# phi(K) as one maximum in place of a clamp and a sum, in a linear attention and GLU block

## The chip, the cores and the metric

One core of a Trainium2 chip. The time is the device time of one execution in microseconds (us); the median of several runs counts. The engines of the core work side by side, each through its own list of instructions in order: TensorE (PE; PEld is its loading of weights), VectorE (DVE), ScalarE (ACT), GpSimd (POOL) and SyncE (SP), which issues transfers. They wait for each other by semaphores.

## The reference

Two pre-norm residual blocks on x of 1 x 2048 x 448, bf16: linear attention with 16 heads of 28, then a gated GELU layer of width 1792.

```python
phi = lambda t: jnp.where(t > 0, t + 1, jnp.exp(t)) + 1e-6
pq, pk = phi(q), phi(k)
kv = jnp.einsum("bhsd,bhse->bhde", pk, v)
z = jnp.einsum("bhsd->bhd", pk)
num = jnp.einsum("bhqd,bhde->bhqe", pq, kv)
den = jnp.einsum("bhqd,bhd->bhq", pq, z)[..., None] + 1e-6
h = x + (num / den) @ wo                  # q, k, v from layernorm(x) @ wqkv
h2 = h + (gelu(g) * u) @ w_down           # g, u from layernorm(h)
```

## The kernel before

The 2048 rows are 16 tiles of 128 rows; tile t holds every 16th row. The program writes down tasks, each with an engine, the buffers it reads and writes, and a name; the five strings of ORDERS give, as task numbers, the order of the tasks on each engine, and waits are derived from the buffers. Where one instruction has several waits, the table HOLD can say whose wait stands first. An instruction never overtakes another on its engine, so a waiting instruction holds up all that stands behind it there.

**Normalization.** For each tile VectorE takes the statistics (L413, L414) and ScalarE the reciprocal deviation (L420, with the pointer eps_t as bias, and L422, without a pointer). The normalized tile xnn has 512 columns: 448 of data and 64 that hold 1.0. The first four tiles are transposed by TensorE with the matrix ident (L443), the others by a transfer (L455), into xnT: four blocks of 128 rows, where rows 64 to 127 of the last block are the ones.

**K and Q tiles.** Task k_t is four matmuls of 448 columns (L469) into one of four PSUM banks that K and Q tiles take in turn; a bank is free again when its tile was read. The weights wqk_sb have zeros in rows 64 to 127 of their last block (L364), so the ones add nothing. ek_t (L480, ScalarE) writes e1 = exp(K); ck_t (L481, VectorE) clamps e1 to between 0 and 1 + 1e-6, in place; pk_t (L482, VectorE) writes max(K, 1e-6) + e1, which is phi(K), to pk in bf16. q_t is the same projection for Q; ScalarE writes exp and relu of it (eq_t L496, rq_t L497), and VectorE later makes phi(Q) of them (cq L564, aq L565).

**P.** The matmuls of L488 multiply xnn, transposed, with pk, and sum over all tiles in four more banks: P = xnn^T pk, 448 rows and one of ones, which gives z. For tiles 10 and later they are split in two tasks: pt1_t, the bank with z, and pt3_t, the three others.

**From P to the output of the attention.** z1 (L514, ScalarE) and z0 (L515, VectorE) put z on all partitions of zbc; evpD_3 (L516, VectorE), evpA_0 and evpA_1 (L519, ScalarE) and evpD_2 (L521, VectorE) copy P to pt_sb in bf16. kv (L527, TensorE) needs all four copies; then kvm (L531), and the task w2 (L547) multiplies with wo; evwA (L551, ScalarE) and evwD (L553, VectorE) evacuate it. For the first two pairs of tiles the denominator goes through t1d or t1p (L569), dr (L572, VectorE), deA (L574, ScalarE, bias by the pointer eps_d), rd (L575) and pn (L576). For tiles 0 and 1 TensorE transposes the result (tro, L599), which takes the banks that w2 used.

The orders around this place, by names:

```
TensorE  ... k_15 pt1_11 pt3_11 pt1_12 pt1_13 pt3_12 pt1_14 pt1_15 pt3_13 pt3_14 pt3_15 q_5 q_4 kv q_7 q_8 w2_2 w2_0 w2_1 q_9 w2_3 tro_1 tro_0 q_6 ...
ScalarE  ... ek_14 ek_15 z1 evpA_0 evpA_1 deA_0 eq_5 eq_4 rq_5 deA_1 deA_2 eq_7 rq_4 deA_3 rq_7 evwA_0 evwA_2 rq_9 ...
VectorE  ... ck_15 pk_15 aq_3 cq_1 evpD_3 z0 aq_1 t1d_0 dr_0 evpD_2 rd_0 dr_1 dr_2 kvm rd_2 kvd dr_3 rd_1 pn_0 rd_3 pn_1 evwD_1 ...
```

**The GLU layer.** After the residual sum and the second normalization, tasks gu (L731, L733: gate and up side by side on half the rows each), ge (L751, gelu on ScalarE, writes gl), hm (L753, product on VectorE, writes hh) and down (L697, L678) follow in chunks of tiles to the end; two pairs of banks alternate for gu, so the third task, gu2_2, needs the first pair read by ge and hm.

Of the kernel before, what the change touches and what calls it, by code (L numbers as in the profile page):

```python
# [5 lines left out]
BF16 = mybir.dt.bfloat16  # L6
F32 = mybir.dt.float32
ALU = mybir.AluOpType
AF = mybir.ActivationFunctionType
# [39 lines left out]
)  # L49
HOLD = {  # L50
    66: (36,), 141: (140,), 165: (164,), 214: (213,), 216: (215,), 323: (302,), 326: (324,), 431: (340,), 704:
    (564,), 735: (734,), 781: (672,), 839: (836,), 849: (846,), 854: (852,), 866: (865,),
# [176 lines left out]
def bass_sequential_preLN__linear_attn_block__glu_gated_geglu__prompt_kernel(  # L229
    nc, A_x, A_wqkv, A_wo, B_x, B_w_gate, B_w_up, B_w_down, out  # L230
):
    S, D, FF, H, DH = 2048, 448, 1792, 16, 28
    T, P = S // 128, S // 256
# [4 lines left out]
    EPS_LN, EPS = 1e-5, 1e-6  # L238
    XN_R, PK_R, HN_R, HR = 10, 8, 4, 8
# [7 lines left out]
    G = _Graph()  # L247
    es = ExitStack()
    with es:
        block = es.enter_context(nc.Block())  # L250

        def sb(name, shape, dt):
            return es.enter_context(nc.sbuf_tensor(name, shape, dt))
# [28 lines left out]
        pk = sb("pk", [128, PK_R, D], BF16)  # L282
# [7 lines left out]
        eps_d = sb("eps_d", [128, 1], F32)  # L290
        rd = sb("rd", [128, 4, H], F32)
# [16 lines left out]
        b_xn = bufs("xn", XN_R)  # L308
# [7 lines left out]
        b_epsd = _Buf("epsd")  # L316
# [33 lines left out]
        def op(eng, fn, r, w, name, after=()):  # L350
            return G.add(eng, fn, r=r, w=w, name=name, after=after)
# [8 lines left out]
        def dma_x(q, a, b):  # L360
            return dma(q, x_sb[:, a:b, :], xv[:, a:b, :], b_x[a:b], "dx%d" % a)

        for dst, b, nm_ in ((wqk_sb, b_wpad[0], "wqkpad"), (wv_sb, b_wpad[1], "wvpad")):
            op("dve", lambda e, dst=dst: e.memset(dst[B_, 3, :], 0.0), [], [b], nm_)  # L364
        dma_x("sp", 0, 1)
# [17 lines left out]
        op("pool", lambda e: e.memset(eps_d[:], EPS), [], [b_epsd], "epsd")  # L383
        op("pool", lambda e: e.memset(mhalf[:], -0.5), [], [b_mhalf], "mhalf")
# [14 lines left out]
        def act_exp(fn, r, w, name):  # L399
            t_ = G.add("act", fn, r=r, w=w, name=name, after=[tbl1])  # L400
            exps.append(t_)
            return t_
# [69 lines left out]
        def proj_reads(t, b):  # L472
            return [(b_xnT[t][0], 0), (b_xnT[t][1], 2), (b[0], 0), (b[1], 3), (b_wpad[0], 3)]

        def k_tile(t):
            bk = slot()
            i, ip = t % 4, t % PK_R
            psK = ps[:, bk, 0:D]
            G.add("pe", lambda e, W: proj(e, W, t, bk, D), r=proj_reads(t, b_wk), w=[b_ps[bk]], name="k_%d" % t, mw=True)
            eks.append(act_exp(lambda e: e.activation(e1[:, i, :], psK, AF.Exp), [b_ps[bk]], [b_e1[i]], "ek_%d" % t))  # L480
            op("dve", lambda e: e.tensor_scalar(e1[:, i, :], e1[:, i, :], 1.0 + EPS, 0.0, ALU.min, ALU.max), [b_e1[i]], [b_e1[i]], "ck_%d" % t)  # L481
            op("dve", lambda e: e.scalar_tensor_tensor(pk[:, ip, :], psK, EPS, e1[:, i, :], ALU.max, ALU.add), [b_ps[bk], b_e1[i]], [b_pk[ip]], "pk_%d" % t)  # L482
            groups = ((3, 0, 1, 2),) if t < PT_SPLIT else ((3,), (0, 1, 2))
            for cs in groups:
                def fpt(e, cs=cs):
                    ins = None
                    for c in cs:
                        ins = e.matmul(ps[:, BK_PT[c], 0:D], xnn[:, t % XN_R, c * 128:(c + 1) * 128], pk[:, ip, :], start=(t == 0), stop=(t == T - 1))  # L488
                    return ins
                G.add("pe", fpt, r=[b_xn[t % XN_R], b_ones2, b_pk[ip]], w=[b_ps[BK_PT[c]] for c in cs], name="pt%d_%d" % (len(cs), t))  # L490
# [23 lines left out]
        op("act", lambda e: e.activation(zbc[B_, :], ps[B_, BK_PT[3], 0:D], AF.Identity), [b_ps[BK_PT[3]]], [b_z[1]], "z1")  # L514
        op("dve", lambda e: e.tensor_copy(zbc[A_, :], zbc[B_, :]), [b_z[1]], [b_z[0]], "z0")  # L515
        op("dve", lambda e: e.tensor_copy(pt_sb[A_, 3, :], ps[A_, BK_PT[3], 0:D]), [b_ps[BK_PT[3]]], [b_pt[3]], "evpD_3")  # L516
        for c in range(3):
            if c in (0, 1):
                op("act", lambda e, c=c: e.activation(pt_sb[:, c, :], ps[:, BK_PT[c], 0:D], AF.Identity), [b_ps[BK_PT[c]]], [b_pt[c]], "evpA_%d" % c)  # L519
            else:  # L520
                op("dve", lambda e, c=c: e.tensor_copy(pt_sb[:, c, :], ps[:, BK_PT[c], 0:D]), [b_ps[BK_PT[c]]], [b_pt[c]], "evpD_%d" % c)  # L521
# [301 lines left out]
```

## Time and profile before

| what | value |
|---|---|
| median of 3 runs | 190.59 us (190.52 to 190.61) |
| span of the profiled execution, first to last instruction | 188.3 us |
| granted TensorE clock in it | 1.000 |
| VectorE, busy in it | 129.3 us |
| ScalarE, busy in it | 76.5 us |

The span is that of one execution; a run's time also holds what lies before the first and after the last instruction. Views that follow: the *chain* goes back from the last instruction to what released each step (columns: start, us, what). The *timeline* gives start, us, engine, line, operation, out<-in and count, and in brackets the idle time before and what ended it; neighbouring instructions of a line are merged. *Windows* give, for a stretch, its length, then busy time and count of each engine, the granted clock, the transfer engines' busy share and GB/s. *Groups* give busy us, mean ns of one, and idle us before. *Waits* give us in total, times, and the longest.

### The profile page before, as it was taken

What the parts mean: (1) busy time and instruction counts of PE and PEld (TensorE: products, weight loads), DVE (VectorE), ACT (ScalarE), POOL (GpSimd) and SP (SyncE); (2) the same over time, 40 slices, a digit from 0 to 9 for tenths busy, and PEclk for the clock granted to TensorE, in tenths of its full rate; (3) what the DMA queues carried; (4) which work ended last, traced back from release to release, by engine and by line L of the source; (5) the groups of instructions that cost most, each with busy time, mean ns of one, the idle gap of its engine ahead of it and who ended that gap; (6) DMA issues with size and microseconds to landing.
All of it is one profiled execution on the core that took longest, in us unless ns stands there. A gap on an engine that the chain in (4) does not pass through costs nothing.

```text
span 188.3 us, 4459 instructions
## 1 busy us (share of the span) xinstructions
PE 184.3 (98%) x1813; PEld 109.2 (58%) x1813; DVE 129.3 (69%) x330; ACT 76.5 (41%) x220; POOL 50.0 (27%) x91
## 2 busy tenths in 40 slices
PE   7999999999999999999999999999999999999994
PEld 7545555555688788965554555555545545454554
DVE  4999959999899998786796762562645244335432
ACT  3878752799963231432234222321242222224100
POOL 6067910704505686033614000206100000000000
PEclk9999999999999999999999999999999999999999
DMA  5996458999393526820005720000096000002024
GB/s 169 387 231 88 96 104 194 218 222 174 65 320 64 95 52 116 84 52 0 0 3 98 144 54 0 0 3 2 3 135 111 3 0 24 3 0 98 3 79 140
DMA packets 35076, 17.11 MB, mean 91 GB/s; under 512 B 26864, under 2 KB 33648, under 8 KB 35056
## 3 DMA queue, kind: packets, MB, share of 16 engines
q1 hardware_dynamic: 34432, 16.32, 41.1%
q10 hardware_dynamic: 624, 0.52, 0.8%
q8 instruction: 14, 0.23, 0.5%
q14 instruction: 6, 0.05, 0.1%
HBM read 8.26 MB, written 1.84 MB: 54 GB/s over the span
## 4 chain that ended last, share of the span: by engine, by line
PE 94%; DVE 3%; DMA 1%; issue 0%
PE ps L733 38%; PE ps L697 19%; PE ps L469 12%; PE ps L731 9%; PE ps L488 6%; PE ps L627 3%; PE ps L678 3%; PE ps L628 2%; DMA x_sb<-in_A_x_dram 1%; DVE st L413 1%; PE ps L617 1%; PE ps L547 1%; PE ps L527 1%; PE ps L443 0%; PE ps L654 0%; DVE den L572 0%
## 5 line engine op out<-in xcount | busy, mean ns | idle before, releaser
L733 PE MATMUL ps<-hnT,wgu_sb 64*128 64x512 bf16 (+1 forms) x490 | 88.8, 333 | 0.0
L731 PE MATMUL ps<-hnT,wgu_sb 64*128 64x512 bf16 (+1 forms) x490 | 88.6, 333 | 0.0
L751 ACT ACTIVATE gl<-ps 128x256 bf16<-128x256 f32 x112 | 36.6, 383 | 85.3 <-PE ps L731 84.4
L753 DVE TENSOR_TENSOR hh<-ps,gl 128x256 bf16<-128x256 f32 x112 | 42.1, 416 | 41.4 <-ACT gl L751 41.3
L733 PEld LDWEIGHTS ps<-hnT,wgu_sb 64*128 64x128 bf16 x490 | 45.2, 94 | 32.9 <-DVE hh L753 3.4
L731 PEld LDWEIGHTS ps<-hnT,wgu_sb 64*128 64x128 bf16 x490 | 45.4, 94 | 2.5
L697 PE MATMUL ps<-wd_sb,hh 64*128 64x448 bf16 x392 | 41.5, 349 | 0.0
L697 PEld LDWEIGHTS ps<-wd_sb,hh 64*128 64x128 bf16 x392 | 23.2, 94 | 14.5
L469 PE MATMUL ps<-wqk_sb,xnT 128*128 128x448 bf16 x128 | 27.4, 353 | 0.0
L413 DVE BATCH_NORM_STATS2 st<-x_sb 128x6 f32<-128x448 bf16 x32 | 19.2, 612 | 1.8 <-DMA x_sb<-in_A_x_dram 1.7
L585 POOL TENSOR_TENSOR t<-pq,zbc 128x448 f32<-128x448 bf16 x12 | 12.3, 1042 | 23.7 <-DVE pq L583 22.0
L469 PEld LDWEIGHTS ps<-wqk_sb,xnT 128*128 128x128 bf16 x128 | 11.9, 98 | 11.4 <-DVE pk L482 0.8
L488 PE MATMUL ps<-pk,xnn 128*128 128x448 bf16 x64 | 13.9, 352 | 0.0
L627 PE MATMUL ps<-w,pqnT 64*128 64x448 bf16 x49 | 11.5, 349 | 0.1
L425 POOL TENSOR_SCALAR ln<-mv 128x2 f32<-128x2 f32 x7 | 2.0, 291 | 35.2 <-DVE mv L414 35.0
L480 ACT ACTIVATE e<-ps 128x448 bf16<-128x448 f32 x16 | 8.5, 539 | 5.6 <-PE ps L469 5.5
L628 PE MATMUL ps<-pt_sb,pqnT 64*128 64x448 bf16 x42 | 10.2, 350 | 0.0
L633 DVE TENSOR_TENSOR x_sb<-ps,x_sb 128x448 bf16<-128x448 f32 x16 | 9.6, 616 | 0.7 <-PE ps L628 0.6
L662 POOL TENSOR_SCALAR hn<-x_sb,nm,rs 128x448 bf16<-128x448 bf16 x14 | 9.9, 719 | 0.4
L482 DVE SCALAR_TENSOR_TENSOR pk<-ps,e 128x448 bf16<-128x448 f32 x16 | 9.8, 617 | 0.1
L488 PEld LDWEIGHTS ps<-pk,xnn 128*128 128x128 bf16 x64 | 6.3, 98 | 5.9 <-DVE pk L482 0.3
L453 POOL TENSOR_SCALAR xnn<-x_sb,nm,rs 128x448 bf16<-128x448 bf16 x12 | 8.9, 744 | 2.2 <-ACT rs L422 1.9
(85 smaller groups left out, 160.5 us busy)
## 6 DMA issues: line engine op xcount, KB each, us to landing
out_dram<-x_sb SPq DMA_DIRECT2D x15, 112.0 KB, 1.8
wd_sb<-in_B_w_down_dram SPq DMA_DIRECT2D x1, 1568.0 KB, 8.4
x_sb<-in_A_x_dram SPq DMA_DIRECT2D x3, 448.0 KB, 5.9
wgu_sb<-in_B_w_gate_dram SPq DMA_DIRECT2D x1, 896.0 KB, 12.1
wgu_sb<-in_B_w_up_dram SPq DMA_DIRECT2D x1, 896.0 KB, 16.5
wgu_sb<-in_B_w_gate_dram SPq DMA_DIRECT2D x1, 672.0 KB, 6.1
wgu_sb<-in_B_w_up_dram SPq DMA_DIRECT2D x1, 672.0 KB, 8.5
wo_sb<-in_A_wo_dram SPq DMA_DIRECT2D x1, 392.0 KB, 7.5
```

Source lines behind the costliest of these rows:

```text
L413: op("dve", lambda e: e.bn_stats(st[:, t, :], src_ap), [b_src], [b_st[t]], "bnst%s_%d" % (tag, t))
L469: ins = e.matmul(ps[:, bk, 0:D], xnT[:, t, k, :], wqk_sb[:, k, c0:c0 + D], start=(k == 0), stop=(k == 3))
L488: ins = e.matmul(ps[:, BK_PT[c], 0:D], xnn[:, t % XN_R, c * 128:(c + 1) * 128], pk[:, ip, :], start=(t == 0), stop=(t == T - 1))
L585: op("pool", lambda e, n=n: e.tensor_tensor(t1[:, n, :], pq[:, a + n, :], zbc[:, :], ALU.mult), [b_pq[a + n]] + b_z, [b_t1[n]], "t1p_%d" % ...
L627: e.matmul(ps[:, BK_OUT[0], 0:D], pqnT[ra, i2, sg // 2, :], w2[ra, sg // 2, :], start=(sg == 0), stop=(sg == 5))
L628: ins = e.matmul(ps[:, BK_OUT[1], 0:D], pqnT[rb, i2, 3 + (sg + 1) // 2, :], (w2 if sg == 6 else w2s)[rb, sg // 2, :], start=(sg == 0), sto ...
L662: op("pool", lambda e, t=t, sh=sh: e.tensor_scalar(hn[:, sh, 0:D], x_sb[:, t, :], nm2[:, t:t + 1], rs2[:, t:t + 1], ALU.add, ALU.mult), [b ...
L697: ins = e.matmul(ps[:, bko[half][n], 0:D], hh[rows, j, sl[n]], wd_sb[rows, j, :], start=(j == 0 and (half == 0 or p == 6)), stop=(j == NJ ...
L731: first = e.matmul(psG[:, jj * N:(jj + 1) * N], wgu_sb[A_, k, j * 128:(j + 1) * 128], hnT[A_, ka_, c0:c0 + N], start=(k == 0), stop=(k == ...
L733: ins = e.matmul(psU[:, jj * N:(jj + 1) * N], wgu_sb[B_, k, j * 128:(j + 1) * 128], hnT[B_, kb_, c0:c0 + N], start=(k == 0), stop=(k == NK ...
L751: G.add("act", lambda e, gi=gi, cs_=cs_, psG=psG: e.activation(gl[:, gi, cs_], psG[:, cs_], AF.Gelu_apprx_tanh), r=[b_ps[BK_G[i]]], w=[b_g ...
L753: op("dve", lambda e, dst=dst, srcU=srcU, srcL=srcL: e.tensor_tensor(dst, srcU, srcL, ALU.mult), [b_ps[BK_U[i]], b_glh], [b_ar[j_][t % HR] ...
```

## The change

K gets its 1 in the projection: row 64 of the last weight block, which meets a row of ones, is set to 1.0 for the K half (w1row). So PSUM holds K + 1; ek_t computes exp(K + 1 - 1) with the pointer neg1 as bias; and pk_t is max(min(e1, 1), K + 1) in one instruction, without the 1e-6. The sixteen ck_t are gone. The 1e-6 comes back where P is read: pk has two more columns that hold 1e-6, the matmuls of L488 take one of them along as column 449, and its sum is added to every column of P as P is evacuated, by a per-partition operand: on VectorE straight from PSUM (evpD_3, evpD_2), on ScalarE as a bias from the new buffer ecol, which VectorE copies out of PSUM; z gets 2048 x 1e-6 from eps_s. The orders of all engines stay; the new tasks stand as follows: w1row behind the two memsets on VectorE, ecol on VectorE between dr_0 and evpD_2, three memsets (neg1, pkeps, epss) in GpSimd's start. The task numbers of ORDERS shift, and HOLD now has some hundreds of entries, mostly the neighbouring task's.

```diff
-        pk = sb("pk", [128, PK_R, D], BF16)
+        pk = sb("pk", [128, PK_R, D + 2], BF16)
...
+        neg1 = sb("neg1", [128, 1], F32)
+        eps_s = sb("eps_s", [128, 1], F32)
+        ecol = sb("ecol", [128, 2], F32)
...
+        op("dve", lambda e: e.memset(wqk_sb[64:65, 3, D:2 * D], 1.0), [b_wpad[0]], [b_w1r], "w1row")
...
+        op("pool", lambda e: e.memset(neg1[:], -1.0), [], [b_neg1], "neg1")
+        op("pool", lambda e: e.memset(eps_s[:], S * EPS), [], [b_epss], "epss")
+        op("pool", lambda e: e.memset(pk[:, :, D:D + 2], EPS), [], [b_pke], "pkeps")
...
-            eks.append(act_exp(lambda e: e.activation(e1[:, i, :], psK, AF.Exp), [b_ps[bk]], [b_e1[i]], "ek_%d" % t))
-            op("dve", lambda e: e.tensor_scalar(e1[:, i, :], e1[:, i, :], 1.0 + EPS, 0.0, ALU.min, ALU.max), [b_e1[i]], [b_e1[i]], "ck_%d" % t)
-            op("dve", lambda e: e.scalar_tensor_tensor(pk[:, ip, :], psK, EPS, e1[:, i, :], ALU.max, ALU.add), [b_ps[bk], b_e1[i]], [b_pk[ip]], "pk_%d" % t)
+            eks.append(act_exp(lambda e: e.activation(e1[:, i, :], psK, AF.Exp, bias=neg1[:, 0:1]), [b_ps[bk], b_neg1], [b_e1[i]], "ek_%d" % t))
+            op("dve", lambda e: e.scalar_tensor_tensor(pk[:, ip, 0:D], e1[:, i, :], 1.0, psK, ALU.min, ALU.max), [b_ps[bk], b_e1[i]], [b_pk[ip]], "pk_%d" % t)
...
-                        ins = e.matmul(ps[:, BK_PT[c], 0:D], xnn[:, t % XN_R, c * 128:(c + 1) * 128], pk[:, ip, :], start=(t == 0), stop=(t == T - 1))
+                        ins = e.matmul(ps[:, BK_PT[c], 0:D + 1], xnn[:, t % XN_R, c * 128:(c + 1) * 128], pk[:, ip, 0:D + 1], start=(t == 0), stop=(t == T - 1))
...
-        op("act", lambda e: e.activation(zbc[B_, :], ps[B_, BK_PT[3], 0:D], AF.Identity), [b_ps[BK_PT[3]]], [b_z[1]], "z1")
+        op("dve", lambda e: e.tensor_copy(ecol[:, 0:2], ps[:, BK_PT[0]:BK_PT[0] + 2, D]), [b_ps[BK_PT[0]], b_ps[BK_PT[1]]], [b_ecol], "ecol")
+        op("act", lambda e: e.activation(zbc[B_, :], ps[B_, BK_PT[3], 0:D], AF.Identity, bias=eps_s[B_, 0:1]), [b_ps[BK_PT[3]], b_epss], [b_z[1]], "z1")
...
-        op("dve", lambda e: e.tensor_copy(pt_sb[A_, 3, :], ps[A_, BK_PT[3], 0:D]), [b_ps[BK_PT[3]]], [b_pt[3]], "evpD_3")
+        op("dve", lambda e: e.tensor_scalar(pt_sb[A_, 3, :], ps[A_, BK_PT[3], 0:D], ps[A_, BK_PT[3], D:D + 1], None, ALU.add), [b_ps[BK_PT[3]]], [b_pt[3]], "evpD_3")
...
-                op("act", lambda e, c=c: e.activation(pt_sb[:, c, :], ps[:, BK_PT[c], 0:D], AF.Identity), [b_ps[BK_PT[c]]], [b_pt[c]], "evpA_%d" % c)
+                op("act", lambda e, c=c: e.activation(pt_sb[:, c, :], ps[:, BK_PT[c], 0:D], AF.Identity, bias=ecol[:, c:c + 1]), [b_ps[BK_PT[c]], b_ecol], [b_pt[c]], "evpA_%d" % c)
...
-                op("dve", lambda e, c=c: e.tensor_copy(pt_sb[:, c, :], ps[:, BK_PT[c], 0:D]), [b_ps[BK_PT[c]]], [b_pt[c]], "evpD_%d" % c)
+                op("dve", lambda e, c=c: e.tensor_scalar(pt_sb[:, c, :], ps[:, BK_PT[c], 0:D], ps[:, BK_PT[c], D:D + 1], None, ALU.add), [b_ps[BK_PT[c]]], [b_pt[c]], "evpD_%d" % c)
```

More of the change, by code (lines that the diff above doesn't have):

```diff
@@ L15 @@
 ORDERS = (
[33 rows of a table removed]
[33 rows of a table added]
 )
 HOLD = {
-    66: (36,), 141: (140,), 165: (164,), 214: (213,), 216: (215,), 323: (302,), 326: (324,), 431: (340,), 704:
-    (564,), 735: (734,), 781: (672,), 839: (836,), 849: (846,), 854: (852,), 866: (865,),
[78 rows of a table added]
 }
@@ L315, in bass_sequential_preLN__linear_attn_block__glu_gated_geglu__prompt_kernel @@
             _Buf(n) for n in ("ident", "ones", "mones", "mtmp", "mask", "eps", "mhalf", "powtmp"))
-        b_epsd = _Buf("epsd")
+        b_epsd, b_epss, b_ecol, b_neg1, b_pke, b_w1r = _Buf("epsd"), _Buf("epss"), _Buf("ecol"), _Buf("neg1"), _Buf("pke"), _Buf("w1r")
         b_st1, b_mv1, b_nm1, b_ln1, b_rs1 = bufs("st1", T), bufs("mv1", T), bufs("nm1", T), bufs("ln1", T), bufs("rs1", T)
@@ L472, in proj_reads @@
         def proj_reads(t, b):
-            return [(b_xnT[t][0], 0), (b_xnT[t][1], 2), (b[0], 0), (b[1], 3), (b_wpad[0], 3)]
+            return [(b_xnT[t][0], 0), (b_xnT[t][1], 2), (b[0], 0), (b[1], 3), (b_wpad[0], 3)] + ([(b_w1r, 3)] if b is b_wk else [])
         def k_tile(t):
@@ L487, in fpt @@
                     for c in cs:
-                        ins = e.matmul(ps[:, BK_PT[c], 0:D], xnn[:, t % XN_R, c * 128:(c + 1) * 128], pk[:, ip, :], start=(t == 0), stop=(t == T - 1))
+                        ins = e.matmul(ps[:, BK_PT[c], 0:D + 1], xnn[:, t % XN_R, c * 128:(c + 1) * 128], pk[:, ip, 0:D + 1], start=(t == 0), stop=(t == T - 1))
                     return ins
-                G.add("pe", fpt, r=[b_xn[t % XN_R], b_ones2, b_pk[ip]], w=[b_ps[BK_PT[c]] for c in cs], name="pt%d_%d" % (len(cs), t))
+                G.add("pe", fpt, r=[b_xn[t % XN_R], b_ones2, b_pke, b_pk[ip]], w=[b_ps[BK_PT[c]] for c in cs], name="pt%d_%d" % (len(cs), t))
         def q_tile(t):
```

144 rows, old and new, of tables (HOLD, ORDERS) are left out of this document.

## The prediction

> **What bounds the kernel now.** I read the page's head and its chain of work first: who sets the end?
>
> ```profile
> span 188.3 us, 4459 instructions
> PE 184.3 (98%) x1813; PEld 109.2 (58%) x1813; DVE 129.3 (69%) x330; ACT 76.5 (41%) x220; POOL 50.0 (27%) x91
> PE 94%; DVE 3%; DMA 1%; issue 0%
> ```
>
> TensorE carries 94% of the chain that ended last. A busy share does not prove that matmuls run at their peak, so I took the stage where the removed instruction lives, between two points of the chain, by windows, and then the waits of TensorE there.
>
> ```profile
> 10.92:32.70 21.78, 21.78 (x117) 11.05 (x115) 19.26 (x56) 13.85 (x42) 10.58 (x26) 1.00 0.65 126
> PEld ps L469 <- DVE pk L482: 0.8, 3, 0.3
> PEld ps L488 <- DVE pk L482: 0.3, 2, 0.2
> ```
>
> 115 weight loads in 21.78 us are 189.4 ns for each 448-column matmul, 0.42 ns a column, at granted clock 1.00 and without a hole; the chain holds nothing but matmuls there. The 1.1 us in which weight loads waited for pk are waits of the loader, hidden behind the matmul in flight: they cost no matmul time. VectorE is busy for 19.26 of these 21.78 us and yet not the bound.
>
> The chain leaves TensorE once, where the sums P are evacuated:
>
> ```profile
> 30.61 2.09 PE ps L488 x11
> 32.73 0.62 DVE pt_sb L516
> 33.37 0.40 DVE zbc L515
> 33.79 0.39 DVE pq L565
> 34.19 0.55 DVE t L569
> 34.76 0.62 DVE den L572
> 35.38 0.54 DVE pt_sb L521
> 35.96 1.03 PE ps L527 x16
> 36.99 1.51 PE ps L469 x8
> ...
> 40.59 0.45 PE ps L599 x8
> ```
>
> TensorE finishes pt1_15 at 32.70; from there VectorE does evpD_3, z0, aq_1, t1d_0, dr_0, evpD_2 back to back, and kv starts at 35.96 when evpD_2 is done. The timeline says how much TensorE loses to this, and where ScalarE stands:
>
> ```profile
> 32.73 0.54 ACT L514 ACTIVATE zbc<-ps 64x448 f32<-64x448 f32 x1 [1.54 <-PE ps L488]
> ...
> 34.23 1.68 PE L469 MATMUL ps<-wqk_sb,xnT 128*128 128x448 bf16 x8
> ...
> 34.43 0.98 ACT L519 ACTIVATE pt_sb<-ps 128x448 bf16<-128x448 f32 x2 [1.16 <-PE ps L488]
> ...
> 35.29 0.61 DVE L521 CAST pt_sb<-ps 128x448 bf16<-128x448 f32 x1
> 35.41 0.31 ACT L574 ACTIVATE den<-den,eps_d 128x16 f32<-128x16 f32 x1
> ...
> 35.82 0.24 DVE L575 RECIPROCAL rd<-den 128x16 f32<-128x16 f32 x1
> ...
> 36.47 0.55 ACT L497 ACTIVATE pq<-ps 128x448 bf16<-128x448 f32 x1
> ```
>
> q_5 and q_4 keep TensorE busy to 34.23 + 1.68 = 35.91, and kv follows 0.05 us later: evpD_2 comes just in time, and evpA_0 and evpA_1 on ScalarE end at 35.41, half a microsecond early. That half microsecond is all the room the change has here.
>
> **The change part by part.** Durations come from these groups:
>
> ```profile
> L420 ACT ACTIVATE ln<-mv,eps_t 128x1 f32<-128x1 f32 x18 | 5.2, 294 | 2.2 <-DVE mv L414 2.0
> ...
> L481 DVE TENSOR_SCALAR e<-e 128x448 bf16<-128x448 bf16 x16 | 4.2, 271 | 2.3 <-ACT e L480 2.2
> ...
> L422 ACT ACTIVATE rs<-ln 128x1 f32<-128x1 f32 x18 | 3.4, 200 | 0.3
> ...
> L435 DVE TENSOR_SCALAR xnn<-x_sb,mv,rs 128x448 bf16<-128x448 bf16 x4 | 1.5, 377 | 0.1
> ...
> L647 DVE COPY hn<-hn 128x64 bf16<-128x64 bf16 x2 | 0.2, 142 | 0.0
> ```
>
> *Removed:* sixteen ck, 16 x 271 ns = 4.3 us of VectorE, all before 32.7 us. They pay nothing: TensorE runs there without a hole, and kv's chain starts at 32.73 from pt1_15, which TensorE reaches in its order after 11 matmuls (30.61 + 2.09), whether pk_15 is early or not. pk itself stays one pass over the same shapes.
>
> *Bias pointer on the sixteen ek:* an ACTIVATE of one column with a pointer bias (L420) takes 294 ns, without one (L422) 200. I take +94 ns for each, the functions being different; bounds 0 and 94. 16 x 94 ns = 1.5 us of ScalarE, while it is busy for 13.85 of 21.78 us, and pk, which follows ek, has lost the 271 ns of ck in between: nothing on the path. Without that room, each would delay pk by its 94 ns.
>
> *Weight row, memsets, 449th column:* w1row writes 448 elements of one partition; the zero memset of 448 words took 0.43 us.
>
> ```profile
> 1.18 0.43 DVE L364 MEMSET wqk_sb<- 64x448 uint32 x1
> ...
> 3.01 0.29 POOL L380 TENSOR_SCALAR_AFFINE_SELECT ident<-ones_bf 128x128 bf16<-128x128 bf16 x1
> ...
> 3.34 0.63 DVE L413 BATCH_NORM_STATS2 st<-x_sb 128x6 f32<-128x448 bf16 x1 [1.73 <-DMA x_sb<-in_A_x_dram]
> ...
> 5.25 0.27 PEld L443 LDWEIGHTS ps<-ident,xnn 128*128 128x128 bf16 x4
> ```
>
> It ends near 2.1 us, inside the 1.73 us in which VectorE waits for x; uncovered it would cost its 0.43. GpSimd's three small memsets lie among its start-up work, whose first urgent result is ident: ready at 3.30, first used by TensorE at 5.25, so 1.95 us cover them. 64 matmuls of 449 columns instead of 448: 64 x 0.42 ns = 0.03 us on the path.
>
> *The evacuations.* This is what matters. evpA_0 and evpA_1 now take their bias from ecol, and ecol stands on VectorE behind dr_0 and ahead of evpD_2. So ScalarE, in order, cannot start evpA_0 at 34.43. Step by step:
> - evpD_3 reads its addend through a pointer. L435 with two pointers takes 377 ns against 271 for L481 with none: 53 ns a pointer, bounds 0 and 0.1. z1, 94 ns longer, ends at 33.36, before evpD_3 (33.40), so z0 goes by evpD_3. ecol's turn: 35.29 + 0.05 = 35.34.
> - ecol itself, two columns out of PSUM, is in no row. The small copy L647 gives 0.14, the reciprocal of 16 columns (0.24, above) the other bound; I take 0.15, since it is a copy: 35.49.
> - To ScalarE 0.05 (evpD_2 ended at 35.90, kv started at 35.96): 35.54.
> - Two evacuations 0.98, plus 2 x 0.094 for the pointers: 1.17. They end at 36.71; kv at 36.77 instead of 35.96: **+0.81 us**. evpD_2, ended near 36.1, is no longer what kv waits for.
>
> *The table HOLD* reorders waits that stand before one instruction; the last to hold decides in either order: 0, or one hand-over of 0.05 us where it does not.
>
> The Trainium skill (VectorE: DVE Perf Modes, section on the TRN2 errata) gives (120 + columns) cycles at 0.96 GHz from PSUM to SBUF, an estimate of 0.13 us for ecol; by it kv would start 0.02 us sooner. No run here shows such a small copy yet.
>
> *What is queued behind.* ScalarE starts deA_0 at 36.71 instead of 35.41, 1.30 late; rd_0 on VectorE waits for it (36.71 + 0.31 + 0.04 = 37.06, 1.24 late), and everything behind it on VectorE. Rows of what follows (the timeline, then ScalarE's window with its busy time second, the first gelu, hm, and gu2_2 in the chain):
>
> ```profile
> 37.93 0.61 DVE L572 TENSOR_REDUCE den<-t 128x16 f32<-128x448 f32 x1
> ...
> 38.65 0.31 ACT L574 ACTIVATE den<-den,eps_d 128x16 f32<-128x16 f32 x1
> ...
> 39.30 0.98 ACT L551 ACTIVATE w<-ps 128x448 bf16<-128x448 f32 x2
> ...
> 40.33 0.53 PEld L599 LDWEIGHTS ps<-ident,pqn 128*128 128x128 bf16 x8 [0.18 <-ACT w L551]
> ...
> 34.40:52.41 18.01, 17.53 (x41) 1.00 0.89 169
> ...
> 52.41 0.66 ACT L751 ACTIVATE gl<-ps 128x256 bf16<-128x256 f32 x2
> ...
> 53.10 0.76 DVE L753 TENSOR_TENSOR hh<-ps,gl 128x256 bf16<-128x256 f32 x2
> ...
> 54.12 0.11 PE ps L733
> ```
>
> ScalarE's reads of the Q tiles shift too: rq_5 ends at 37.02 + 1.30 = 38.32, and q_8, which takes its bank, comes at 36.77 + 1.03 + 0.76 = 38.56, so it need not wait. dr_3 ends 1.24 late at 39.78, so deA_3 starts at 39.82 instead of 38.65, and the evacuations of w2 end at 40.28 + 1.17 = 41.45. The transposes tro wait for these (they did already, by 0.18 us, hidden): weight load at 41.50, first matmul near 41.60 instead of 40.59. TensorE is **1.0 us** late, 0.2 more than at kv. From 34.40 to 52.41 ScalarE has 18.01 - 17.53 = 0.48 us of idle time, so the first gelu comes 0.8 to 1.0 late, hm with it, and gu2_2, which started 0.26 us after hm ended (53.86 to 54.12), finds no more than the 1.0 that TensorE already has. From there on TensorE is at full pace to the end and cannot make it up.
>
> **Sum.** 0.81 + 0.2 + 0.03 = +1.03 us on the span, 188.3 to 189.3. The runs' median is 190.59, 2.3 us above the span for what lies around it: **191.6**. Ends: no pointer cost, ecol 0.14, to ScalarE 0.03, no lateness added behind: kv 0.53 late, 191.1. Evacuation pointers 0.1, ecol 0.24, and TensorE inheriting ScalarE's whole lateness, 1.5: 192.1.
>
> **The rivals.**
> - *Faster: VectorE was holding TensorE after all.* If the loader's waits for pk (0.8 + 0.3 us) were lost matmul time, freeing VectorE by 4.3 us would return them, and the evacuation would have to hide too: 190.59 - 1.1 = 189.5. It decides before 32.7 us. For it: VectorE's 19.26 of 21.78 us. Against it: 189.4 ns a matmul without a hole. The Trainium skill (Perfetto Trace Analysis, Identifying the Most-Contended Engine) holds matmul busy time a bad measure and would look at weight loads, here 58%; by that rule TensorE has room and this rival gains. The trace's pace does not bear it out.
> - *No change: the wait is paid but regained.* That needs slack on TensorE behind kv. The chain shows matmuls end to end from 40.59; I find only the 0.05 before kv. Time 190.6 to 190.9.
> - *Slower by more: the odd 449th column costs a step.* If such a matmul ran as long as 512 columns, 64 x 63 x 0.42 ns = 1.7 us more: 193.3. No row here has an odd width. By the Trainium skill (VectorE: DVE Perf Modes, errata table), a matmul costs 6 + columns cycles, which has no such step.
>
> **How the numbers follow.** Forecast 0.84, faster 0.04, no change 0.07, the step 0.05. The range, 190.9 to 192.4, takes in the forecast's own ends (191.1, 192.1) and 0.2 to 0.3 us on each side, for sums of several rows and for what a late ScalarE may do further on. 0.2% (0.38 us) is about what a measurement of this kernel can tell from no change: slower 0.89, same 0.07, faster 0.04.
>
> **What would show it.** Right: evpA_0 idle until ecol, starting near 35.5; kv near 36.8 with a hole of about 0.9 us on TensorE before it, released by ScalarE's pt_sb; the chain going through ScalarE there; ek near 630 ns; 10.9 to 32.7 us unchanged on TensorE, with the loader's waits for pk gone. Wrong: kv before 36.4, matmuls L488 paced above 190 ns, or TensorE reaching 10.92 or 32.7 earlier than now.

## The result, and the profile after

| | before | after |
|---|---|---|
| median of ten runs each | 190.64 us | 191.23 us |
| ratio after / before | | 1.0036 [1.0023, 1.0049] |
| span of the profiled execution | 188.3 us | 189.2 us |

The change makes the kernel slower by 0.36%, some 0.7 us (0.44 to 0.93 by the interval). One of the ten runs of the changed kernel took 244.72 us at a granted clock of 0.757; the ratio leaves it out, and the median is the same without it. The prediction said slower, 191.6 us; the direction and the place were right, the sum 0.3 us too large. The head of the changed kernel's page:

```profile
span 189.2 us, 4449 instructions
PE 184.8 (98%) x1813; PEld 109.8 (58%) x1813; DVE 126.8 (67%) x316; ACT 77.4 (41%) x220; POOL 49.6 (26%) x94
...
PE 96%; DVE 2%; ACT 1%; issue 0%; POOL 0%; POOLq 0%
```

VectorE lost 2.5 us of work (129.3 to 126.8) and nothing came of it; ScalarE is new on the chain, with 1%. First the stage in which the clamps were, by windows, and then the waits:

```profile
10.92:32.70 21.78, 21.78 (x117) 11.21 (x116) 16.30 (x41) 14.86 (x42) 10.31 (x26) 1.00 0.66 128
```

```profile
PEld ps L552 <- DVE pk L564: 0.3, 1, 0.3
```

VectorE's busy time fell from 19.26 to 16.30 us, ScalarE's rose from 13.85 to 14.86; the loader's waits for pk fell from 1.1 to 0.3 us; and TensorE is what it was, 21.78 of 21.78 us with 116 weight loads for 115. What was taken from VectorE was never on the path. Next the chain around P:

```profile
30.74 2.11 PE ps L570 x11
...
34.97 0.62 DVE den L655
35.59 0.08 DVE ecol L596
...
35.69 1.17 ACT pt_sb L602 x2
...
36.90 1.03 PE ps L610 x16
...
41.53 0.45 PE ps L682 x8
```

Down to dr_0 (den L655) its steps are those of before. Then it goes by ecol to ScalarE, and the two evacuations on it, 1.17 us, now stand end to end between P and kv. In the kernel before they ran beside VectorE's t1d_0 and dr_0 and were half a microsecond early. The timeline shows what that costs each engine:

```profile
34.39 1.68 PE L552 MATMUL ps<-wqk_sb,xnT 128*128 128x448 bf16 x8
...
35.51 0.15 DVE L596 COPY ecol<-ps 128x2 f32<-128x2 f32 x1
35.58 0.68 DVE L604 TENSOR_SCALAR pt_sb<-ps 128x448 bf16<-128x448 f32 x1
35.69 1.16 ACT L602 ACTIVATE pt_sb<-ps,ecol 128x448 bf16<-128x448 f32 x2 [2.19 <-DVE ecol L596]
...
36.90 1.03 PE L610 MATMUL ps<-pt_sb,wv_sb 128*112 128x112 bf16 x16 [0.84 <-ACT pt_sb L602]
...
37.25 1.08 DVE L655 TENSOR_REDUCE den<-t 128x16 f32<-128x448 f32 x2
...
38.98 0.61 DVE L655 TENSOR_REDUCE den<-t 128x16 f32<-128x448 f32 x1
...
40.27 0.96 ACT L634 ACTIVATE w<-ps 128x448 bf16<-128x448 f32 x2
```

q_4 ends at 34.39 + 1.68 = 36.07 and kv starts at 36.90: a hole of 0.84 us, released by ScalarE. evpD_2 (L604) has been done since 36.26. From kv on, the lateness neither grows nor shrinks: kv is 0.94 us later than before (35.96), the transposes tro start at 41.53 in the chain, 0.94 us later than before (40.59), and the last output sum on VectorE starts at 186.85 instead of 185.90, 0.95 later. The durations that the prediction had to estimate:

```profile
L570 PE MATMUL ps<-pk,xnn 128*128 128x449 bf16 x64 | 14.0, 353 | 0.0
...
L563 ACT ACTIVATE e<-ps,neg 128x448 bf16<-128x448 f32 x16 | 9.9, 631 | 5.3 <-PE ps L552 5.0
...
L602 ACT ACTIVATE pt_sb<-ps,ecol 128x448 bf16<-128x448 f32 x2 | 1.2, 630 | 2.2 <-DVE ecol L596 2.2
...
L599 DVE TENSOR_SCALAR pt_sb<-ps 64x448 bf16<-64x448 f32 x1 | 0.7, 680 | 0.3 <-PE ps L570 0.3
...
L596 DVE COPY ecol<-ps 128x2 f32<-128x2 f32 x1 | 0.1, 149 | 0.0
```

### The profile page after: what moved, and what is told of

Read it like the earlier page. It is cut to its first block, busy times and chain, and to the rows that moved or that the text cites. A ratio compares the mean times of both kernels' runs of the same rounds, so it can differ in the third digit from the quotient of the medians.

```text
span 189.2 us, 4449 instructions
## 1 busy us (share of the span) xinstructions
PE 184.8 (98%) x1813; PEld 109.8 (58%) x1813; DVE 126.8 (67%) x316; ACT 77.4 (41%) x220; POOL 49.6 (26%) x94
## 4 chain that ended last, share of the span: by engine, by line
PE 96%; DVE 2%; ACT 1%; issue 0%; POOL 0%; POOLq 0%
PE ps L816 38%; PE ps L780 19%; PE ps L552 12%; PE ps L814 8%; PE ps L570 6%; PE ps L710 3%; PE ps L761 3%; PE ps L490 2%; PE ps L711 2%; PE ps L700 1%; PE ps L526 1%; PE ps L630 1%; ACT pt_sb L602 1%; PE ps L610 1%; PE ps L737 0%; DVE pt_sb L599 0%
## 5 line engine op out<-in xcount | busy, mean ns | idle before, releaser
L570 PE MATMUL ps<-pk,xnn 128*128 128x449 bf16 x64 | 14.0, 353 | 0.0
L564 DVE SCALAR_TENSOR_TENSOR pk<-e,ps 128x448 bf16<-128x448 bf16 x16 | 9.6, 612 | 5.1 <-ACT e L563 5.1
L563 ACT ACTIVATE e<-ps,neg 128x448 bf16<-128x448 f32 x16 | 9.9, 631 | 5.3 <-PE ps L552 5.0
```

Source lines behind the costliest of these rows:

```text
L570: ins = e.matmul(ps[:, BK_PT[c], 0:D + 1], xnn[:, t % XN_R, c * 128:(c + 1) * 128], pk[:, ip, 0:D + 1], start=(t == 0), stop=(t == T - 1))
```

## The experiments

The stage of K and Q tiles ends a little earlier or later in each execution, by up to 0.2 us mostly and by up to 1 us when x or a transposed tile lands late (below). So each place is given by its distance from one earlier point, the first of the eleven matmuls that lead to pt1_15 (30.61 before, 30.74 after; in e3, e4, e11 and e12, whose chains run on in TensorE, these matmuls open a run of twenty). "kv" and "tro" are the starts of these tasks in the chain, less that point (kv of e4 and e12, whose chains pass it by, is from the timeline); "end" is the start of the last output sum on VectorE, the chain's last step, less the same point. Ratios are times against the kernel before, run beside it on the same chip.

| kernel | kv | tro | end | ratio |
|---|---|---|---|---|
| before | 5.35 | 9.98 | 155.29 | 1 |
| after | 6.16 | 10.79 | 156.11 | 1.0036 [1.0023, 1.0049] |
| e8, after again | 6.16 | 10.79 | 156.10 | 1.0051 [1.0033, 1.0069] |
| e6, after, exp without pointer | 6.16 | 10.79 | 156.10 | 1.0044 [1.0027, 1.0062] |
| e9, after, evacuations without pointer | 5.97 | 10.62 | 155.98 | 1.0044 [1.0028, 1.006] |
| e2, before with the wait | 5.88 | 10.48 | 155.79 | 1.0042 [1.0029, 1.0054] |
| e2b, the same again | 5.88 | 10.48 | 155.79 | 1.0015 [1.0003, 1.0027] |
| e5, after, ecol one place up | 5.55 | 10.15 | 155.46 | 1.0004 [0.999, 1.0018] |
| e3, phi(K) alone | 5.41 | 10.02 | 155.33 | 1.0006 [0.9991, 1.0021] |
| e1, before without the clamp | 5.36 | 9.99 | 155.30 | 1.0003 [0.9989, 1.0016] |
| e4, after, reordered | 5.96 | 11.00 | 156.51 | 1.0058 [1.0042, 1.0073] |
| e12, e4 with GpSimd behind VectorE | 5.25 | 10.28 | 155.79 | 1.0022 [1.001, 1.0035] |
| e10, before with late x | 5.35 | 9.99 | 155.30 | 1.004 [1.0023, 1.0056] |
| e11, phi(K) alone with late x | 5.41 | 10.01 | 155.32 | 1.0042 [1.0029, 1.0056] |

In this table the scatter of the start is taken out, which the ratios still hold. Behind tro every kernel but e4 and e12 keeps its lateness to the end within 0.05 us; those two lose another 0.2 us.

**The clamp alone.** In the kernel before, ck is taken out and nothing else is done, so the clamp is missing from the result.

```diff
-            op("dve", lambda e: e.tensor_scalar(e1[:, i, :], e1[:, i, :], 1.0 + EPS, 0.0, ALU.min, ALU.max), [b_e1[i]], [b_e1[i]], "ck_%d" % t)
```

> The kernel before without the sixteen ck: the clamp of exp(K) is left out of the result, nothing else moves. My theory (TensorE has no hole there, VectorE's 4.3 us are cover): time as before, 190.6 within 0.1, TensorE from its first pt4_0 to pt1_15 in 21.8 us as before, the loader's waits for pk gone. Rival (VectorE was holding TensorE): about 189.5, 1.1 us less.

Its windows, and its start of kv in the chain:

```profile
10.92:32.70 21.78, 21.78 (x117) 11.25 (x115) 16.19 (x41) 13.68 (x42) 10.23 (x26) 1.00 0.66 127
```

```profile
30.59 2.10 PE ps L488 x11
...
35.95 1.03 PE ps L527 x16
```

Ratio 1.0003, kv 0.01 us from where it was. 3.1 us less of VectorE in this stage (4.3 by the count of 16 x 271 ns; rows that follow each other overlap in the trace) are worth nothing that can be measured, which settles the rival "VectorE was holding TensorE". The Trainium skill (Perfetto Trace Analysis, section Identifying the Most-Contended Engine) would have TensorE's headroom judged by MFU and by weight-load busy time, 58% here; the run shows that this headroom can't be had by relieving VectorE.

**The wait alone.** The kernel before, where evpA_0 waits for dr_0. No ecol, no pointers.

```diff
+        by = {t.name: t for t in G.all}
+        G.dep(by["evpA_0"], [by["dr_0"]])
         G.place(ORDERS)
```

> The kernel before with one wait added: evpA_0 also waits for dr_0, as ecol makes it do in the changed kernel. No ecol, no pointers, no other change. My theory: evpA_0 starts near 35.4 instead of 34.4, the pair ends 0.98 later at 36.4, kv starts at 36.45, 0.5 late, and nothing is regained: 191.1 (190.9 to 191.3). Rival (regained behind kv): 190.6 to 190.7.

> The kernel before with evpA_0 waiting for dr_0, a second time. The first time its time was 1.0042 (1.0029 to 1.0054) of the kernel before, more than the 0.5 us expected, and in its profile x for tiles 4 to 7 came at 8.40 us, so that VectorE set the pace to 18.5 us; past that point kv was late by the 0.53 expected. If the late x is scatter: tiles 4 to 7 on time in this profile, kv 0.5 late, and about 191.0 (1.0026). If the added wait costs more than its place shows: kv again 0.5 late but the time again 191.3 or more.

The second run's timeline:

```profile
35.33 0.61 DVE L523 CAST pt_sb<-ps 128x448 bf16<-128x448 f32 x1
35.44 0.98 ACT L521 ACTIVATE pt_sb<-ps 128x448 bf16<-128x448 f32 x2 [2.14 <-DVE den L574]
...
36.52 1.00 PE L529 MATMUL ps<-pt_sb,wv_sb 128*112 128x112 bf16 x16 [0.58 <-DVE pt_sb L523]
```

kv is 0.53 us late in both. The timeline names VectorE's evpD_2 (L523) as releaser, which ended at 35.94; the evacuations ended at 35.44 + 0.98 = 36.42, so it was ScalarE. The wait on VectorE's place in its list is thus two thirds of the 0.81. The two ratios, 1.0042 and 1.0015, don't overlap although the delay is the same; the first run's profile has the end of the K stage 0.9 us late (the eleven matmuls at 31.54), and that led to e10.

**The pointers.** First the evacuations wait for ecol but don't read it (the 1e-6 is left out in the two blocks); then the exp of K loses its pointer (its -1 is left out).

```diff
-... AF.Identity, bias=ecol[:, c:c + 1]), [b_ps[BK_PT[c]], b_ecol], [b_pt[c]], "evpA_%d" % c)
+... AF.Identity), [b_ps[BK_PT[c]], b_ecol], [b_pt[c]], "evpA_%d" % c)
```

> The changed kernel with evpA_0 and evpA_1 still waiting for ecol, but without the bias pointer, so the 1e-6 is left out of these two blocks of P. My theory: the pair takes 0.98 instead of 1.16, kv 0.19 sooner than in the changed kernel (near 36.7 where it was 36.90), 191.05. Rival (the pointer costs nothing on the path): kv unmoved, 191.2.

```diff
-... AF.Exp, bias=neg1[:, 0:1]), [b_ps[bk], b_neg1], [b_e1[i]], "ek_%d" % t))
+... AF.Exp), [b_ps[bk]], [b_e1[i]], "ek_%d" % t))
```

> The changed kernel with exp without its pointer bias; so the result holds exp(K + 1) and the -1 is left out. The changed kernel's TensorE reached pt4_0 at 11.03 instead of 10.92 and pt1_15's end at 32.85 instead of 32.70. If the pointer's 94 ns on ek_0 and ek_1 (which stand ahead of the copies of the transposed tiles 2 and 3 on ScalarE) make the 0.11: 10.92 again, and 191.1, 0.1 below the changed kernel. If it is scatter of the start: still about 11.0, time as the changed kernel, 191.2.

e9's chain:

```profile
31.52 2.11 PE ps L570 x11
...
36.46 0.99 ACT pt_sb L602 x2
...
37.49 1.03 PE ps L610 x16
```

kv comes 0.19 us sooner than in the changed kernel: 6.16 to 5.97, two pointers of 0.09. At the end 0.12 of it is left (155.98 against 156.10); the ratios don't tell the two apart (1.0044 against 1.0036 and 1.0051, the intervals overlap). e6 has kv at 6.16 like the changed kernel, though its sixteen exp take 541 ns for 631: 16 x 90 ns = 1.4 us of ScalarE lie beside other work. Its eleven matmuls start at 30.59, 0.15 us sooner than in the first profile of the changed kernel; that is not the pointer, since e8, with the pointer, has 30.60.

**phi(K) alone.** The changed kernel without the 449th column, ecol and the addends; the 1e-6 is left out of P.

```diff
-                        ins = e.matmul(ps[:, BK_PT[c], 0:D + 1], xnn[...], pk[:, ip, 0:D + 1], ...)
+                        ins = e.matmul(ps[:, BK_PT[c], 0:D], xnn[...], pk[:, ip, 0:D], ...)
...
-        op("dve", lambda e: e.tensor_copy(ecol[:, 0:2], ps[:, BK_PT[0]:BK_PT[0] + 2, D]), ..., "ecol")
...
-... AF.Identity, bias=ecol[:, c:c + 1]), [b_ps[BK_PT[c]], b_ecol], [b_pt[c]], "evpA_%d" % c)
+... AF.Identity), [b_ps[BK_PT[c]]], [b_pt[c]], "evpA_%d" % c)
...
-... e.tensor_scalar(pt_sb[:, c, :], ps[:, BK_PT[c], 0:D], ps[:, BK_PT[c], D:D + 1], None, ALU.add), ...
+... e.tensor_copy(pt_sb[:, c, :], ps[:, BK_PT[c], 0:D]), ...
```

> The changed kernel with phi(K) as one maximum and the weight row, but without what brings the 1e-6 back into P: no column 449, no ecol, plain evacuations; the 1e-6 is left out of P (z keeps it). My theory (all of the loss is in the evacuations): kv near its old place, at most 0.15 late from the start of the kernel; 190.6 to 190.8. Rival (the loss is in phi(K), the pointer of exp or the weight row): stays at 191.2.

The chain doesn't leave TensorE here:

```profile
30.67 3.79 PE ps L570 x20
34.46 1.51 PE ps L552 x8
35.98 0.11 issue
36.08 1.00 PE ps L609 x16
```

Ratio 1.0006, kv 0.06 us late, the end 0.04. The new phi(K), with its weight row, its exp by a pointer and a HOLD almost as long, costs nothing and pays nothing that the time shows; the loss is in how the 1e-6 is put back.

**The one place that matters.** The changed kernel whole, with ecol moved up by one instruction.

```diff
 VectorE:
-... aq_1 t1d_0 dr_0 ecol evpD_2 rd_0 ...
+... aq_1 t1d_0 ecol dr_0 evpD_2 rd_0 ...
```

> The changed kernel with one task moved: ecol ahead of dr_0 instead of behind it, on VectorE; nothing else. My theory (the place of ecol in VectorE's order sets kv): evpA_0 starts one dr_0 (0.54 us from start to start) sooner, near 35.15 where it was 35.69, and kv comes 0.5 sooner, near 36.4 with evpD_2 close behind; time 190.7 to 190.9, 0.4 to 0.5 below the changed kernel. Rival (the loss lies in pointers or in what comes after kv): within 0.15 of the changed kernel, 191.1 to 191.3.

```profile
34.91 0.15 DVE L596 COPY ecol<-ps 128x2 f32<-128x2 f32 x1
...
35.09 1.16 ACT L602 ACTIVATE pt_sb<-ps,ecol 128x448 bf16<-128x448 f32 x2 [1.53 <-DVE ecol L596]
35.56 0.68 DVE L604 TENSOR_SCALAR pt_sb<-ps 128x448 bf16<-128x448 f32 x1
...
36.34 1.00 PE L610 MATMUL ps<-pt_sb,wv_sb 128*112 128x112 bf16 x16 [0.22 <-ACT pt_sb L602]
```

The evacuations end at 36.25 and evpD_2 at 36.24: ScalarE and VectorE arrive together, and kv is 0.20 us late instead of 0.81. The ratio is 1.0004, no different from before. Every cost of the change but the wait behind dr_0 is still in this kernel.

**Further up, a miss.** If ecol stands ahead of t1d_0, and evpD_2 ahead of dr_0, kv should have no wait left. Further on, rd_3 is put ahead of pn_3 on VectorE and deA_3 behind evwA_2 on ScalarE.

```diff
 VectorE:
-... aq_1 t1d_0 dr_0 ecol evpD_2 rd_0 dr_1 dr_2 kvm rd_2 kvd dr_3 rd_1 pn_0 rd_3 pn_1 ...
+... aq_1 ecol t1d_0 evpD_2 dr_0 dr_1 rd_0 dr_2 kvm rd_2 kvd rd_1 pn_0 pn_1 dr_3 ...
 ScalarE:
-... evpA_0 evpA_1 deA_0 eq_5 eq_4 rq_5 ...
+... evpA_0 evpA_1 eq_5 eq_4 deA_0 rq_5 ...
```

> The whole change with another order from ecol on: VectorE does ecol ahead of t1d_0 and evpD_2 ahead of dr_0, dr_1 ahead of rd_0, rd_1, pn_0 and pn_1 ahead of dr_3, rd_3 ahead of pn_3; ScalarE does eq_5 and eq_4 ahead of deA_0, and deA_3 behind the evacuations of w2. My theory: evpA_0 near 34.75, kv within 0.1 of where q_4 ends, tro on time, time as the kernel before, 190.5 to 190.8. Rival (the change costs time whatever the order): 190.9 or more. It should not beat the kernel before by more than 0.1, since TensorE has no hole to fill.

It came out the slowest, at 1.0058. Its timeline:

```profile
35.20 1.04 POOL L652 TENSOR_TENSOR t<-pq,zbc 128x448 f32<-128x448 bf16 x1 [8.84 <-DVE pq L648]
...
35.38 1.34 DVE L652 TENSOR_TENSOR t<-pq,zbc 128x448 f32<-128x448 bf16 x1
...
36.64 0.68 DVE L604 TENSOR_SCALAR pt_sb<-ps 128x448 bf16<-128x448 f32 x1
...
37.42 1.00 PE L610 MATMUL ps<-pt_sb,wv_sb 128*112 128x112 bf16 x16 [0.64 <-ACT eq L578]
...
37.92 2.04 POOL L652 TENSOR_TENSOR t<-pq,zbc 128x448 f32<-128x448 bf16 x2 [1.68 <-DVE den L655]
...
39.00 0.62 DVE L655 TENSOR_REDUCE den<-t 128x16 f32<-128x448 f32 x1 [0.47 <-POOL t L652]
```

t1d_0 on VectorE takes 1.34 us instead of 0.62. With ecol ahead of it, it starts 0.18 us after GpSimd's product t1p_1, which reads zbc too; in the kernels where t1d_0 started first it took 0.62. There GpSimd's product is the long one, 1.35 us before and after for 1.04 here. evpD_2 then ends at 37.32, and kv, which needs it, starts 0.10 later (the eq that the row names is not among the tasks that kv waits for). By the Trainium skill (SBUF — State Buffer, section Who interferes with whom) a VectorE instruction with two inputs in SBUF contends with a GpSimd one that reads SBUF, and the order of issue decides which of the two is blocked. The trace agrees, with t1d_0 ending 0.48 us after t1p_1 (36.72 against 36.24); a wait to t1p_1's very end and then its own 0.62 would have put it at 36.86.

The chain that ended last doesn't go through kv here. GpSimd's second product, t1p_2, writes over what dr_0 reads; dr_0 stands behind evpD_2 now, and t1p_2 starts only at 37.92. dr_2 on VectorE waits for it, kvm stands behind dr_2, and w2 waits for kvm: tro is 1.02 us late.

The next run takes only the contention away: t1p_1 waits for t1d_0.

```diff
+        by = {t.name: t for t in G.all}
+        G.dep(by["t1p_1"], [by["t1d_0"]])
         G.place(ORDERS)
```

> The kernel e4_reordered with one wait more: GpSimd's t1p_1 starts only after VectorE's t1d_0. In e4_reordered t1d_0, started 0.18 us after t1p_1, took 1.34 us where it takes 0.62 in the changed kernel, in which it starts first; that held evpD_2 and kv back. If the two engines hinder each other by who starts first: t1d_0 takes 0.62 again and kv comes 0.4 to 0.6 sooner after pt1_11's start than in e4_reordered (5.96 there, 5.4 to 5.6 here). If t1d_0 is long for another reason (ecol in front of it): 1.3 again, kv at 5.9 to 6.0. For the time I expect 190.8 to 191.5 in the first case, since dr_1 and what follows come later, 191.5 in the second.

```profile
34.85 0.62 DVE L652 TENSOR_TENSOR t<-pq,zbc 128x448 f32<-128x448 bf16 x1
...
35.55 3.16 POOL L652 TENSOR_TENSOR t<-pq,zbc 128x448 f32<-128x448 bf16 x3 [9.72 <-DVE t L652]
...
36.18 1.03 PE L610 MATMUL ps<-pt_sb,wv_sb 128*112 128x112 bf16 x16
...
37.74 0.62 DVE L655 TENSOR_REDUCE den<-t 128x16 f32<-128x448 f32 x1 [0.27 <-POOL t L652]
...
38.95 1.31 PE L630 MATMUL ps<-wo_sb,hh 112*128 112x448 bf16 x6 [0.23 <-DVE hh L614]
```

t1d_0 is back at 0.62, 0.72 us less than in e4; kv starts at 36.18, 5.25 behind the point, even earlier than in the kernel before, and tro is 0.72 sooner than in e4. The rest of e4's price stays where it was: dr_2 on VectorE waits for GpSimd's second product, kvm stands behind dr_2, and w2 waits for kvm. tro is 0.30 us late, the end 0.50, and the ratio 1.0022. The second product is late for two reasons that end together and that this run can't tell apart: the first product, started at 35.55 behind t1d_0, ends at 36.59, and dr_0, behind evpD_2, at 36.60.

**The scatter.** e2's first profile had the x of tiles 4 to 7 land 0.4 us late. Was that why its times were higher, and would a kernel without clamps make up for it? The transfer of these tiles is put behind two loads of weights, in the kernel before and in phi(K) alone; and the changed kernel is run once more beside them.

```diff
-        dma_x("sp", 4, 8)
         dma_w1("sp", wqk_sb, 0, D, b_wq, "dw1_t")
+        dma_w3("sp", wv_sb, 2 * D, 3 * D, b_wv, "dwv")
+        dma_x("sp", 4, 8)
...
-        dma_w3("sp", wv_sb, 2 * D, 3 * D, b_wv, "dwv")
```

> The kernel before with x of tiles 4 to 7 issued behind two weight loads on SyncE's queue (the remaining rows of the Q weights and wv), so that it comes later, by an estimate 0.5 to 1.5 us, about as late as in one profile of the added wait. My theory: VectorE, with the statistics of tiles 4 and on queued behind that transfer, is then the bound up to about 18 us, and the time grows by about as much as x is late, to 191.3 or more.

> phi(K) as one maximum without the 1e-6 brought back into P, with x late as in the kernel e10. My theory: without the clamps VectorE catches up, since each tile costs it 0.27 us less, so it loses less than e10 does: 0.4 us or more below e10. Rival (the clamps never pay): the same time as e10 within 0.15.

> The changed kernel as it is, for a second profile and a second comparison: 191.2 (1.0025 to 1.0045); kv 0.8 after the end of q_4 again; the start of TensorE's pt4_0 within 0.15 of 10.92, wherever x lands.

e10's timeline row for the first of these tiles, whose statistics started at 8.02 in the kernel before, and its chain:

```profile
9.04 0.63 DVE L415 BATCH_NORM_STATS2 st<-x_sb 128x6 f32<-128x448 bf16 x1 [1.05 <-DMA x_sb<-in_A_x_dram]
```

```profile
31.63 2.10 PE ps L490 x11
...
36.98 1.03 PE ps L529 x16
```

x comes 1.02 us late (9.04 for 8.02), the K stage ends 1.02 late (31.63 for 30.61), and the median rises to 191.37 against 190.54. So a late x is paid in full at the end of this stage, and can raise a time by as much as the change does. That the kernel without clamps would catch up was my theory, and it fell: e11 has 1.0042 to e10's 1.004, and its eleven matmuls start at 31.70, with x at 9.15; from x to there it gains 0.04 us on e10. The freed time on VectorE pays nothing that the time shows even then. e2's 0.9 us is more than the 0.4 by which x was late there. TensorE lost most of the rest in one more wait, 0.36 us for k_6 at 18.52. The chain names a statistic on VectorE for it, which k_6 does not read; of the tasks that k_6 does wait for, exp and pk of tile 4 were done at 17.82, which leaves the transfer of its transposed tile. Such a transfer can be late with x on time: in e4's profile tile 4's statistics start at 8.15, TensorE waits 0.57 us for a transposed tile at 15.38, and the eleven matmuls start at 31.46. The changed kernel again: kv at 6.16 to the hundredth.

## Why the prediction was right, and where its sum was off

- *The bound.* TensorE from 10.92 to 32.70 us without a hole, whatever VectorE does: shown by the windows of after and by e1. The forecast that the loader's waits for pk would be gone was not quite so: 0.3 us of 1.1 are left, hidden like the others.
- *The sixteen exp* were to take 94 ns more each and cost nothing: 631 ns against 539, and e6 shows the nothing.
- *The start-up, HOLD and the 449th column.* w1row took 0.43 us, to 2.20, and VectorE still waited 1.00 us for x behind it. HOLD cost no more than one hand-over: phi(K) alone, with a HOLD of 619 entries for 621, has kv 0.06 us late. The eleven matmuls took 2.11 us for 2.09. No step at 449 columns, 353 ns each; the rival at 193.3 us is out.
- *The evacuations, +0.81 us at kv.* This term came out to the hundredth: 6.16 less 5.35, three times, and not by errors that cancel: in e8 ecol ended at 35.51 (35.49 forecast), the evacuations at 36.71 (36.71) and kv started at 36.76 (36.77). Its parts, by e2b and e8: the wait alone 0.53; the evacuations start another 0.15 later (35.55 - 30.60 in e8, 35.44 - 30.64 in e2b), 0.07 of it by evpD_3's pointer and 0.08 by ecol, the part of it that does not overlap dr_0; they take 0.19 longer; and kv follows 0.05 sooner on their end. ecol took 149 ns, 0.15 forecast. The Trainium skill (VectorE: DVE Perf Modes, section on the TRN2 errata) gave an estimate of 0.13 for it; the measurement differs, by 0.02 us, and decides.
- *The pointer on VectorE* costs 63 ns: evpD_3 took 680 ns as an add by a pointer, 617 as a plain copy. 53 was taken.
- *The knock-on, +0.2 us at tro: the term that was mis-sized.* It measured 0: tro is late by 10.79 - 9.98 = 0.81, what kv is late by and no more, and the end by 0.82. The step that failed is "dr_3 ends 1.24 late at 39.78". It carried rd_0's whole lateness down VectorE's list. But in the kernel before, dr_1 and dr_2 took 1.29 us together, and after the change 1.08 (37.25, above). GpSimd's products in the timelines of before and after:

```profile
34.27 3.39 POOL L569 TENSOR_TENSOR t<-pq,zbc 128x448 f32<-128x448 bf16 x3 [8.83 <-DVE pq L565]
```

```profile
34.49 2.35 POOL L652 TENSOR_TENSOR t<-pq,zbc 128x448 f32<-128x448 bf16 x2 [8.85 <-DVE pq L648]
37.89 1.04 POOL L652 TENSOR_TENSOR t<-pq,zbc 128x448 f32<-128x448 bf16 x1 [1.05 <-DVE den L655]
```

Before, the second product ended at 36.62 (34.27 + 3.39 less 1.04 for the third), when dr_1 was done, and dr_2 had to wait for it. After, the second ended at 36.84 (34.49 + 2.35), before dr_1 began, and dr_2 waited for nothing. Less the 0.13 us by which this execution was late from its start, rd_0 came 1.13 late (37.08 for 35.82; 1.24 forecast), dr_3 0.92 (38.98 for 37.93; 1.24 forecast), and the evacuations of w2 0.84 (40.27 for 39.30; 1.17 forecast): in time for tro. A lateness was carried through a wait that could use it up: 1.29 less 1.08 is the 0.21 between 1.13 and 0.92. The first 0.11 were deA_0's, which started at 36.74, when the row of the evacuations still ran to 36.85; in the kernel before the two met at 35.41.
- *The rest.* kv in the profiled execution stood at 36.90 where 36.77 was forecast; the other 0.13 lies ahead of the change (30.74 for 30.61). In e8 and e6 these matmuls started at 30.60 and 30.59, so it is the scatter of the start. Without the knock-on the sum is 0.81 + 0.03 = 0.84, inside the measured 0.44 to 0.93 and near the 0.82 at the end of the trace; with it, 1.03, it is outside.
- *No change: paid but regained.* tro and the end (0.95 late in the profiled execution, of which 0.13 were there at the start) show that nothing is regained behind kv; in e2b, e5, e6, e8 and e9 no more than 0.03 us of kv's lateness is gone at the end.

## What to carry to other kernels

An instruction that makes a value cheaper can be worth nothing on an engine that the bound does not wait for; look first for holes in the bound's own row. A tiny new operand for another engine is priced by its place in the list: here two columns of copy behind one reduction used up a 0.5 us margin and cost 0.8 us more, and one place further up gave 0.6 us of it back. When you carry a lateness along an engine, subtract each wait on a third engine that it meets on the way.

## What was not expected of the hardware

The same product on VectorE took 0.62 us, or 1.34 us when GpSimd had begun its own 0.18 us earlier (e4, e12), and GpSimd's product took 1.35 us instead of 1.04 when VectorE had begun first, so that an order can lose without any wait. The first transfers scatter: the statistics of tile 4 started at 8.02 in the kernel before, with x there, and at 8.42 in e2, after a wait for it, though the programs are the same up to there. TensorE did not catch up in any profile (in the table, e2 and e2b have the same end behind points 0.9 us apart), so the whole kernel shifts with it; two measurements of one kernel gave 1.0042 and 1.0015. To place a cost of half a microsecond, distances within the trace were worth more than the times.
